# Linear attention and two expert layers: the order of the first head pair's token groups, omega's preparation, and matmuls over zeros at the start

## The chip, the cores and the metric

One Trainium2 chip, one core of it. A NeuronCore has a matrix engine (TensorE, PE in the profile, with its weight loads as PEld), VectorE (DVE), ScalarE (ACT), GpSimd (POOL) and SyncE (SP), which here issues the loads and stores. Each engine works through its own queue in order and waits on semaphores for the others. The metric is the time of one execution on the device in microseconds (us); lower is better.

## The reference

Attention with random features, then a layer with h - tanh(h), then four experts weighted by probabilities. Sizes: batch 2, 8 heads, 576 tokens, head width 64, 128 features; 1152 tokens by 512 channels in both layers.

```python
def phi(x):
    proj = np.einsum('bhsd,md->bhsm', x, omega)
    sq = np.sum(x * x, axis=-1, keepdims=True) / 2.0
    h = proj - sq
    h = h - np.max(h, axis=-1, keepdims=True)
    return np.exp(h) / np.sqrt(m)
q_p, k_p = (phi(q_s), phi(k_s))             # q and k scaled by D**-0.25
kv = np.einsum('bhsm,bhsd->bhmd', k_p, v)
z = np.sum(k_p, axis=2)
num = np.einsum('bhsm,bhmd->bhsd', q_p, kv)
den = np.einsum('bhsm,bhm->bhs', q_p, z)[..., None] + 1e-06
x = num / den                               # 1152 x 512
h = x @ w_in
x = (h - np.tanh(h)) @ w_out
for e in range(4):
    out += p[:, e:e + 1] * (np.maximum(x @ w1[e], 0.0) @ w2[e])
```

## The kernel before

The eight heads are taken as four pairs. A pair's keys are 2 x 576 tokens. In tiles of 128 rows that is nine: four full tiles of each batch, and one tile that holds the last 64 tokens of both batches, the rest. `kn` holds a pair's full tiles (two loads, one for each batch), `kr` the rests of all pairs, `vs0` and `vs1` the values of the even and odd pairs, `qn` and `qr` the queries. SyncE issues every load, in program order; a load into a buffer that is used again waits until the last reader of the buffer is done: the values of pair 2 wait for the products of pair 0 (in two halves, one for each batch), the keys of pair 3 for the transposes of pair 1.

`features` (lines 273 to 306) turns a pair's keys into features in two kinds of step. `transposed` turns four blocks of 128 x 128 at a time by matmuls with `ident` into `psT` (two buffers, line 284) and splits the result into a rounded half `th` (ScalarE, line 71) and the remainder `tl` (VectorE, line 72). `projected` takes one group: two token tiles of both heads, or the rest tile. For each block of 128 columns it does three matmuls of 256 columns (line 296: `th` by `ob0`, `th` by `ob1`, `tl` by `ob0`) into `psP`, which has two buffers; then VectorE takes the maximum (`nm`, line 298) and ScalarE the exponentials into `kf`, one for each tile and head (line 302). The buffer of `psP` comes free behind the last exponential. The list `groups` says in which order tiles are taken: two groups of batch 0, the rest, two groups of batch 1.

`k_products` (line 308) multiplies features and values: 20 products of a pair into `psV` (line 314), each of which is two records in the trace. Behind the keys the queries go through the same features, `psQ` and `psN` are their further steps, and `pse` and `psh` are the first matmuls of the first layer. The weights of that layer come in as `raw` (line 103), are decoded on ScalarE (`y`, line 111) and VectorE (`m`, lines 122, 126, 127) and are split into `wah` and `wal`.

`ob0` and `ob1` are omega's two parts: omega is loaded (`om`), transposed into `pso` (line 251), scaled into `oms` (line 253) and split (lines 71 and 72) into two tiles that were cleared before (line 256).

In the attention a scheduler of the framework sets the order of the instructions on each engine: it goes by the order of the program and by its own estimate of when operands are ready. From the first `psh` on, the order on TensorE, VectorE and ScalarE is the one that is written in the program.

## Time and profile before

| | us |
|---|---|
| median of 3 runs | 681.08 (680.87 to 681.24) |
| the profiled execution | 681.03 |
| its span, first to last instruction | 678.9 |
| TensorE busy (matmuls) | 666.2, 98% |
| weight loads | 621.5, 92% |
| VectorE busy | 529.8, 78% |
| ScalarE busy | 317.5, 47% |

TensorE is busy nearly all the time, so a part of the kernel matters by how much time TensorE loses in it, by waiting or by a slow clock. A row of the time by stage gives, for a stretch from A to B, the busy time of each engine with its number of instructions, then the granted clock, the share of the DMA engines' time and the rate in GB/s. A row of a timeline begins with its start and its duration; several instructions of one kind in a row are merged (x4), and a bracket at its end tells how long the engine had been idle and what ended that.

### The profile page before, as it was taken

The numbers are of one execution on the slowest core, as the hardware profiler recorded it, in microseconds if no ns is written. First come the engines' busy times: TensorE is split into PE (matmuls) and PEld (weight loads), VectorE is DVE, ScalarE is ACT, GpSimd is POOL, SyncE is SP. The second block draws the span as 40 slices with busy tenths as digits, with TensorE's granted clock in tenths as the row PEclk, the third lists the DMA queues.
The fourth block names the chain that finished last, engine by engine and source line by source line (L and its number), as shares of the span: only waits on it lengthen the run. The fifth ranks groups of instructions, "written<-read, shape, count | busy, mean of one in ns | idle before, by whom it ended". The sixth has DMA issues, their size and how long they took to land.

```text
span 678.9 us, 10154 instructions
## 1 busy us (share of the span) xinstructions
PE 666.2 (98%) x4059; PEld 621.5 (92%) x4059; DVE 529.8 (78%) x828; ACT 317.5 (47%) x593; POOL 62.3 (9%) x58
## 2 busy tenths in 40 slices
PE   6999999999999999999999999999999999999997
PEld 5999989999999999998999999998998999999986
DVE  4599889799999988968377777777777777777664
ACT  5699988857767756444122322222232223222120
POOL 1032023413212200100000000000000000000000
PEclk9999999999999999999999999999999999999999
DMA  8953201122322222121001111210202111110004
GB/s 225 281 169 119 67 32 32 32 62 95 94 63 93 78 79 63 31 63 32 1 31 63 32 49 45 63 33 32 63 31 63 32 63 32 36 58 1 1 0 140
DMA packets 42767, 43.73 MB, mean 64 GB/s; under 512 B 5600, under 2 KB 37600, under 8 KB 42720
## 3 DMA queue, kind: packets, MB, share of 16 engines
q1 hardware_dynamic: 42720, 43.08, 20.7%
q8 instruction: 32, 0.52, 0.3%
q14 instruction: 15, 0.12, 0.1%
HBM read 40.72 MB, written 2.36 MB: 63 GB/s over the span
## 4 chain that ended last, share of the span: by engine, by line
PE 79%; DVE 11%; ACT 5%; issue 2%; DMA 2%; SPq 1%; DVEq 0%
PE po L671 29%; PE Y L654 23%; PE po L550 7%; PE psh L437 7%; PE pse L437 4%; PE psP L296 3%; PE psN L348 2%; DVE m L127 1%; DVE m L126 1%; DVE y L451 1%; DVE y L452 1%; DVE y L454 1%; DVE psh L453 1%; ACT y L448 1%; PE psQ L337 1%
## 5 line engine op out<-in xcount | busy, mean ns | idle before, releaser
L677 DVE SCALAR_TENSOR_TENSOR oacc<-po,pr,oacc 128x512 f32<-128x512 f32 (+1 forms) x136 | 101.4, 746 | 34.3 <-PE po L671 33.8
L671 PE MATMUL po<-wbh,hl 128*128 128x512 f32 x290 | 113.0, 389 | 0.4 <-DVE hl L474 0.4
L671 PE MATMUL po<-wbh,hh 128*128 128x512 f32 x290 | 112.9, 389 | 0.1
L671 PE MATMUL po<-wbl,hh 128*128 128x512 f32 x290 | 112.9, 389 | 0.0
L671 PEld LDWEIGHTS po<-wbh,hl 128*128 128x128 f32 x290 | 54.4, 188 | 12.3 <-DVE hl L474 0.8
L671 PEld LDWEIGHTS po<-wbh,hh 128*128 128x128 f32 x290 | 54.7, 188 | 8.2 <-DVE oacc L677 0.3
L842 ACT ACTIVATE hh<-Y 128x576 fp32r<-128x576 f32 x42 | 27.4, 652 | 72.5 <-DVE Y L839 64.0
L671 PEld LDWEIGHTS po<-wbl,hh 128*128 128x128 f32 x290 | 54.4, 188 | 7.5
L550 PE MATMUL po<-hh,wbh 128*128 128x384 f32 x180 | 60.8, 338 | 0.3
L550 PE MATMUL po<-hl,wbh 128*128 128x384 f32 x180 | 60.7, 337 | 0.3 <-DVE hl L456 0.2
L550 PE MATMUL po<-hh,wbl 128*128 128x384 f32 x180 | 60.4, 336 | 0.0
L654 PE MATMUL Y<-y,wah 128*128 128x288 f32 x336 | 57.9, 294 | 0.0
L437 PE MATMUL psh<-x,wah 128*128 128x384 f32 x288 | 57.7, 336 | 0.0
L654 PEld LDWEIGHTS Y<-y,wah 128*128 128x128 f32 x336 | 51.2, 188 | 3.6 <-DVE hl L474 0.3
L437 PEld LDWEIGHTS psh<-x,wah 128*128 128x128 f32 x288 | 50.5, 188 | 0.0
L654 PE MATMUL Y<-Th,wal 128*128 128x288 f32 x224 | 47.9, 295 | 0.0
L654 PE MATMUL Y<-Tl,wah 128*128 128x288 f32 x224 | 47.6, 294 | 0.0
L654 PE MATMUL Y<-Th,wah 128*128 128x288 f32 x224 | 47.6, 293 | 0.0
L842 ACT ACTIVATE hh<-u 128x576 fp32r<-128x576 f32 x14 | 9.6, 687 | 73.5 <-DVE u L839 73.5
L654 PEld LDWEIGHTS Y<-Th,wah 128*128 128x128 f32 x224 | 39.0, 188 | 4.5
L455 ACT ACTIVATE hh<-y 128x1152 fp32r<-128x1152 f32 (+3 forms) x26 | 20.6, 796 | 41.4 <-DVE y L454 41.4
L624 ACT ACTIVATE wah<-y 128x512 fp32r<-128x512 f32 x28 | 17.6, 631 | 41.1 <-DVE y L604 41.1
(138 smaller groups left out, 1472.7 us busy)
## 6 DMA issues: line engine op xcount, KB each, us to landing
raw<-in_moe_w_dram SPq DMA_DIRECT2D x30, 512.0 KB, 3.5
raw<-in_moe_w_in_dram SPq DMA_DIRECT2D x16, 512.0 KB, 3.6
raw<-in_moe_w_out_dram SPq DMA_DIRECT2D x16, 512.0 KB, 3.4
kn<-in_k_dram SPq DMA_DIRECT2D x8, 256.0 KB, 3.9
vs<-in_v_dram SPq DMA_DIRECT2D x8, 256.0 KB, 4.3
qn<-in_q_dram SPq DMA_DIRECT2D x8, 256.0 KB, 4.9
out_dram<-oacc SPq DMA_DIRECT2D x7, 256.0 KB, 2.2
raw<-in_moe_w_dram SPq DMA_DIRECT2D x4, 256.0 KB, 3.2
```

The source lines that it names most:

```text
L126: nc.vector.scalar_tensor_tensor(out=m, in0=self.y.bitcast(I32), scalar=3, in1=m, op0=ALU.logical_shift_left, op1=ALU.bitwise_or)
L127: nc.vector.scalar_tensor_tensor(out=m, in0=self.up, scalar=SIGN, in1=m, op0=ALU.bitwise_and, op1=ALU.bitwise_or)
L296: nc.tensor.matmul(ps[:, i].rearrange("p a m -> p (a m)"), x[:, c], o, start=j == 0, stop=j == 2)
L348: nc.tensor.matmul(ps[:, j, h, :ZC], qt[g][:, j, h, :], kvz[p][:, t // (TB + 1), h, :], start=True, stop=True)
L437: nc.tensor.matmul(ph[i, j][:, n, :CH] if bank is None else bank, w[:, c], x[:, n * CH:(n + 1) * CH] if bank is None else x[:, n], start=z ...
L455: h=lambda: act.activation(hh, y, AF.Copy),
L550: nc.tensor.matmul(po[:, :CH], w[:, r], g[:, s], start=j == 0 and z == 0, stop=j == NJ - 1 and z == 2,)
L624: nc.scalar.activation(w[0], src, AF.Copy)
L654: nc.tensor.matmul(ps[:, m, :HN // 2], w[:, kk], b[:, m * HN // 2:(m + 1) * HN // 2], start=first and kk == 0 and z == 0, stop=kk == 1 and ...
L671: nc.tensor.matmul(po, g[:, s], w[:, cols], start=j == 0 and z == 0, stop=j == 1 and z == 2)
L677: nc.vector.scalar_tensor_tensor(out=acc, in0=po, scalar=pr[:, t, e:e + 1], in1=acc, op0=ALU.mult, op1=ALU.add)
L842: nc.scalar.activation(halves(gs[NA + q, f][0][:, h * HN:(h + 1) * HN]), x, AF.Relu)
```

## The change

Three edits, all at the start of the attention. `kgroups` gives pair 0 another order of groups: the two of batch 0, the two of batch 1, then the rest; the other pairs keep theirs. Omega's transpose, scaling and split are put under the scheduler's high priority, behind the clearing of `ob`. And twelve matmuls of 256 columns (`busy`, six ahead of omega's transpose and six behind) over a tile of zeros go to a bank of PSUM that nothing reads (`idle`); the tile `zero` is cleared by VectorE first. Of the tag `n` in PSUM `idle` takes one of two buffers, which `psV` uses next.

```diff
--- before.py
+++ after.py
@@ -246,22 +246,36 @@
     load_v(0)
     kn.append(load_k(1))
     load_v(1)
-
-    pso = ps_t.tile([P, 512], F32, tag="t", name="pso")
-    nc.tensor.transpose(pso[:, :P], om.rearrange("p j d -> p (j d)"), ident)
-    oms = kp.tile([P, P], F32, name="oms", bufs=1)
-    nc.scalar.mul(oms, pso[:, :P], scale)
+    zero = kp.tile([P, 2 * P], F32R, name="zero", bufs=1)
+    nc.vector.memset(zero.bitcast(F32), 0.0)
+    idle = ps_n.tile([P, 512], F32, tag="n", name="idle")
+
+    def busy(n):
+
+        for _ in range(n):
+            nc.tensor.matmul(idle[:, :2 * P], zero[:, :P], zero, start=True, stop=True)
+
+
     ob = [ac.tile([P, 2 * P], F32R, name=f"ob{a}") for a in range(2)]
     for a in range(2):
         nc.vector.memset(ob[a].bitcast(F32), 0.0)
-    for j in range(2):
-        r, c = slice(j * D, (j + 1) * D), slice(j * P, (j + 1) * P)
-        split(ob[0][r, c], ob[1][r, c], oms[r, :])
+    pso = ps_t.tile([P, 512], F32, tag="t", name="pso")
+    with tc.high_priority():
+        busy(6)
+        nc.tensor.transpose(pso[:, :P], om.rearrange("p j d -> p (j d)"), ident)
+        busy(6)
+        oms = kp.tile([P, P], F32, name="oms", bufs=1)
+        nc.scalar.mul(oms, pso[:, :P], scale)
+        for j in range(2):
+            r, c = slice(j * D, (j + 1) * D), slice(j * P, (j + 1) * P)
+            split(ob[0][r, c], ob[1][r, c], oms[r, :])
     qn = ac.tile([P, B, H, TD], F32, name="qn")
     kvz = [ac.tile([P, B, 2, ZC], F32, name=f"kvz{p}") for p in range(NP)]
 
 
     groups = [(0, 2), (2, 2), (TB, 1), (TB + 1, 2), (TB + 3, 2)]
+
+    kgroups = [groups[:2] + groups[3:] + groups[2:3]] + [groups] * (NP - 1)
 
     def blocks(full, rest, t0, n):
 
@@ -374,7 +388,7 @@
     post = []
     for p in range(NP):
         kf = kp.tile([P, NT, 2, M], F32, tag="xf", name="kf")
-        T, R = features(lambda b, h: kn[p][:, b, h], kr[:, 2 * p:2 * p + 2, :].rearrange("p h d -> p (h d)"), groups, kf, kp)
+        T, R = features(lambda b, h: kn[p][:, b, h], kr[:, 2 * p:2 * p + 2, :].rearrange("p h d -> p (h d)"), kgroups[p], kf, kp)
         interleave(T[:2] + R[:2] + T[2:] + R[2:], post)
         post = k_products(p, kf)
         if p + 2 < NP:
```

Lines below `kgroups` are 14 further down in the changed program (line 284 is 298, 296 is 310, 314 is 328, 302 is 316, 298 is 312). The scheduler orders the attention anew. From the first `psh` of the first layer on, TensorE's order is the same in both.

TensorE at the start, before: omega (`pso`), four transposes of pair 0's first batch, then the rest `kr` with three of the second batch.

```order
L251 MATMUL pso_126<-ident_67,om_97 128x128
L284 MATMUL psT_146<-ident_67,kn_99 128x128 x4
L284 MATMUL psT_153<-ident_67,kr_102 128x128
L284 MATMUL psT_153<-ident_67,kn_99 128x128 x3
L296 MATMUL psP_160<-ob0_130,th_144 128x256
L296 MATMUL psP_173<-ob0_130,th_144 128x256
L284 MATMUL psT_186<-ident_67,kn_99 128x128
L296 MATMUL psP_160<-ob1_131,th_144 128x256
```

And with the change, the twelve passes first:

```order
L256 MATMUL idle_128<-zero_126 128x256 x12
L265 MATMUL pso_133<-ident_67,om_97 128x128
L298 MATMUL psT_161<-ident_67,kn_99 128x128 x4
L298 MATMUL psT_168<-ident_67,kn_99 128x128 x4
L310 MATMUL psP_175<-ob0_129,th_159 128x256
L310 MATMUL psP_188<-ob0_129,th_159 128x256
L298 MATMUL psT_201<-ident_67,kr_102 128x128
L310 MATMUL psP_175<-ob1_130,th_159 128x256
```

All eight transposes of full tiles now stand ahead of that of `kr`, and the two first projections too.

TensorE further on, where pair 0's last groups meet pair 1 (keys `kn_119` and features `kf_143` before, `kf_158` now) and pair 2 (`kn_240`). Before:

```order
L296 MATMUL psP_211<-ob0_130,th_144 128x256
L296 MATMUL psP_211<-ob1_131,th_144 128x256
L296 MATMUL psP_211<-ob0_130,tl_145 128x256
L296 MATMUL psP_211<-ob0_130,th_144 128x256
L296 MATMUL psP_211<-ob1_131,th_144 128x256
L296 MATMUL psP_211<-ob0_130,tl_145 128x256
L314 MATMUL psV_224<-vs0_105,kf_143 128x128 x4
L284 MATMUL psT_281<-ident_67,kn_119 128x128
L314 MATMUL psV_224<-vs0_105,kf_143 128x128
```

With the change:

```order
L298 MATMUL psT_296<-ident_67,kn_119 128x128
L310 MATMUL psP_231<-ob0_129,th_159 128x256
L310 MATMUL psP_231<-ob1_130,th_159 128x256
L310 MATMUL psP_231<-ob0_129,tl_160 128x256
L298 MATMUL psT_379<-ident_67,kn_240 128x128 x4
L310 MATMUL psP_265<-ob0_129,th_244 128x256
L310 MATMUL psP_265<-ob1_130,th_244 128x256
L310 MATMUL psP_265<-ob0_129,tl_245 128x256
L328 MATMUL psV_239<-vs0_105,kf_158 128x128
```

The rest group (three projections, `psP_231`) is the last of pair 0 now, and the transposes of pair 2's first batch (`psT_379`) stand ahead of pair 1's first projections (`psP_265`); before they stood 20 rows further down.

SyncE's loads from the queries' rests (`qr`) to the first weights (`raw`), before:

```order
L203 DMA qr_338<-in_q_dram 64x8x64 x2
L199 DMA qn_138<-in_q_dram 128x2x256 x2
L199 DMA vs0_105<-in_v_dram 128x2x256
L237 DMA vs0_105<-in_v_dram 64x2x64
L199 DMA kn_335<-in_k_dram 128x2x256 x2
L199 DMA qn_138<-in_q_dram 128x2x256 x2
L199 DMA vs0_105<-in_v_dram 128x2x256
L237 DMA vs0_105<-in_v_dram 64x2x64
L199 DMA qn_138<-in_q_dram 128x2x256 x4
L103 DMA raw_349<-in_moe_w_in_dram 128x4x128
```

With the change:

```order
L203 DMA qr_353<-in_q_dram 64x8x64 x2
L199 DMA kn_350<-in_k_dram 128x2x256 x2
L199 DMA qn_153<-in_q_dram 128x2x256 x3
L199 DMA vs0_105<-in_v_dram 128x2x256
L237 DMA vs0_105<-in_v_dram 64x2x64
L199 DMA qn_153<-in_q_dram 128x2x256 x3
L199 DMA vs0_105<-in_v_dram 128x2x256
L237 DMA vs0_105<-in_v_dram 64x2x64
L199 DMA qn_153<-in_q_dram 128x2x256 x2
L103 DMA raw_364<-in_moe_w_in_dram 128x4x128
```

The keys of pair 3 (`kn_335`, now `kn_350`) and one more load of queries moved ahead of the first values of pair 2 (`vs0`). ScalarE around the first use of `raw`, before:

```order
L302 ACTIVATE kf_361<-psP_383,nm_390 128x128 x4
L302 ACTIVATE kf_361<-psP_401,nm_408 128x128 x3
L111 ACTIVATE y_351<-raw_349 128x512
L302 ACTIVATE kf_361<-psP_401,nm_408 128x128
L302 ACTIVATE kf_361<-psP_423,nm_427 128x128 x2
L71 ACTIVATE th_481<-psT_483 128x512
```

With the change:

```order
L316 ACTIVATE kf_376<-psP_416,nm_423 128x128 x2
L111 ACTIVATE y_366<-raw_364 128x512
L316 ACTIVATE kf_376<-psP_416,nm_423 128x128 x2
L316 ACTIVATE kf_376<-psP_438,nm_442 128x128 x2
L71 ACTIVATE wah_372<-m_368 128x512
L111 ACTIVATE y_485<-raw_483 128x512
```

`y` stood ahead of the last of a group's four exponentials and now stands ahead of the last two of them.

## Rows read from the trace of the kernel before

**Rows 1.** Time by stage: window, busy PE, PEld, DVE, ACT, POOL, clock, DMA.

```profile
11.00:32.00 21.00, 19.88 (x166) 19.21 (x165) 11.86 (x22) 15.46 (x53) 0.00 (x0) 1.00 0.92 274
32.00:51.00 19.00, 18.48 (x157) 17.69 (x155) 18.96 (x33) 17.92 (x52) 6.53 (x5) 1.00 0.60 181
51.00:117.00 66.00, 66.00 (x508) 61.75 (x509) 59.56 (x154) 60.20 (x156) 14.55 (x13) 1.00 0.20 64
117.00:679.00 562.00, 556.94 (x3214) 518.56 (x3213) 436.28 (x612) 220.39 (x328) 38.95 (x28) 1.00 0.16 50
```

**Rows 2.** Timeline of TensorE, 2 to 12 us: start, duration, instruction.

```profile
4.52 1.11 PE L284 MATMUL psT<-ident,kn 128*128 128x128 f32 x4 [1.28 <-DMA kn<-in_k_dram]
7.62 0.45 PE L284 MATMUL psT<-ident,kr 128*128 128x128 f32 x1 [1.99 <-DMA kr<-in_k_dram]
...
10.21 0.41 PE L296 MATMUL psP<-ob,th 128*128 128x256 f32 x1
10.43 0.41 PE L296 MATMUL psP<-ob,tl 128*128 128x256 f32 x1
...
11.09 0.60 PE L284 MATMUL psT<-ident,kn 128*128 128x128 f32 x4
11.52 0.27 PE L284 MATMUL psT<-ident,kr 128*128 128x128 f32 x1
```

**Rows 3.** DMA issues of pair 1's keys, at 6.30 and 6.94: us to landing.

```profile
kn<-in_k_dram SPq DMA_DIRECT2D x1, 256.0 KB, 3.7
...
kn<-in_k_dram SPq DMA_DIRECT2D x1, 256.0 KB, 4.1
```

**Rows 4.** Timeline of all engines, 0 to 60 us: VectorE and ScalarE.

```profile
6.91 0.59 DVE L72 TENSOR_TENSOR ob<-oms,ob 64x128 fp32r<-64x128 f32 x2
...
10.45 1.52 DVE L298 TENSOR_REDUCE nm<-psP 128x4 f32<-128x512 f32 x2 [0.19 <-PE psP L296]
...
11.18 2.17 ACT L302 ACTIVATE kf<-psP,nm 128x128 f32<-128x128 f32 x8 [1.51 <-DVE nm L298]
```

**Rows 5.** Timeline of SyncE's queue, 12 to 32 us.

```profile
12.45 1.13 SPq L199 DMA_DIRECT2D qn<-in_q_dram  x2
16.27 0.37 SPq L199 DMA_DIRECT2D vs<-in_v_dram  x1
...
22.49 2.12 SPq L199 DMA_DIRECT2D qn<-in_q_dram  x4
24.66 0.47 SPq L103 DMA_DIRECT2D raw<-in_moe_w_in_dram  x1
```

**Rows 6.** Time by stage, shorter stretches; the last number is GB/s.

```profile
16.00:18.00 2.00, 2.00 (x21) 2.00 (x19) 1.11 (x3) 1.64 (x7) 0.00 (x0) 1.00 0.67 167
...
28.00:32.00 4.00, 2.92 (x25) 2.67 (x24) 1.69 (x5) 2.90 (x11) 0.00 (x0) 1.00 1.07 338
```

**Rows 7.** DMA issue of the first weights at 24.66: us to landing.

```profile
raw<-in_moe_w_in_dram SPq DMA_DIRECT2D x1, 512.0 KB, 6.0
```

**Rows 8.** The page's DMA issues: all weights of that kind, median to landing.

```profile
raw<-in_moe_w_in_dram SPq DMA_DIRECT2D x16, 512.0 KB, 3.6
```

**Rows 9.** Timeline of ScalarE, 24 to 35 us.

```profile
30.70 0.67 ACT L111 ACTIVATE y<-raw 128x512 f32<-128x512 f32 x1 [1.10 <-DMA raw<-in_moe_w_in_dram]
31.27 0.86 ACT L302 ACTIVATE kf<-psP,nm 128x128 f32<-128x128 f32 x3
```

**Rows 10.** Timeline of TensorE, 26 to 36 us.

```profile
31.68 0.50 PE L296 MATMUL psP<-ob,th 128*128 128x256 f32 x2 [1.08 <-ACT kf L302]
...
33.16 1.05 PE L314 MATMUL psV<-vs,kf 128*128 128x128 f32 x8
34.05 0.27 PE L284 MATMUL psT<-ident,kr 128*128 128x128 f32 x1
```

**Rows 11.** The chain of waits, in order of time: start, us, what.

```profile
30.70 0.68 ACT y L111
...
49.16 0.64 ACT wbh L71
```

## The prediction

> **What bounds the kernel now.** I read the time by stage first [rows 1]. From 117 us on TensorE is busy for 556.94 of 562 us, and the change leaves its order there alone, so that part only shifts as a block: whatever the attention gains or loses before 117 us is the whole effect. The profiled execution took 681.03 us, its span 678.9 and 2.13 around it; the median of the three runs is 681.08, so sums against the profiled one need no correction. Between 11 and 32 us TensorE is busy for 19.88 of 21 us, from 32 to 51 for 18.48 of 19, beside VectorE's 18.96 of 19. Three engines are nearly full, and a gain of one reaches the end only if the others follow.
>
> Next the start [rows 2]. The first transposes begin at 4.52 us, when the keys land. The transpose of the rest (`kr`) waits 1.99 us more, to 7.62, and everything behind it in TensorE's queue waits too. From there TensorE works on, but slowly: the passes of 256 columns at 10.21 and 10.43 are 0.21 us apart, which is 1.2 GHz; the four transposes from 11.09 to 11.52 take 0.11 each, the full clock. The column of the granted clock says 1.00 throughout, so here only the spacing shows the two levels.
>
> Then the keys of pair 1. Their two loads are issued from 6.30 and 6.94 us and take 3.7 and 4.1 us [rows 3], so they land at about 10.0 and 11.04. Before, their transposes begin at 11.09, 0.05 us behind the second landing. **This is the gate at the front:** the slow clock and the wait for `kr` were paid inside the time which that load takes anyway.
>
> **The change part by part.** The passes over zeros: 12 of 0.21 us are 2.5 us, from about 1.2 us (behind a first memset) to 3.8. They delay omega's transpose by about 1 us, which has slack: the ScalarE copies of `ob` stand behind the first `th` copy in both orders, and VectorE's parts of `ob` were done at 7.5 [rows 4]. They end 0.7 us ahead of the keys at 4.52, so they cost nothing; if they began 0.8 us later, they would push the first transposes.
>
> Omega's priority: it moves omega's parts past nothing on ScalarE or VectorE (the same copies stand ahead of them), so I count it as zero.
>
> The rest group last: the second four transposes of pair 0 no longer stand behind `kr`. They need keys issued half a microsecond behind the first, so they run from about 5.4 us in time that was idle. At 7.62 one transpose and ten projections are left. At either clock they end by 10.0 (11 x 0.21 = 2.3) and then the keys of pair 1 are waited for, to 10.0 and 11.04. At 11.06 five transposes more than before are done: 5 x 0.11 = **0.55 us gained**.
>
> From 11 to 22.5 us I set the new order against the rows' durations: transposes 0.11 and matmuls of the products 0.11 each (eight from 33.16 to 34.05, two records to a product), a group of six projections 0.7 (twelve from 31.68 to 33.16) [rows 10], a maximum 0.7 and a group's four exponentials 1.1 [rows 4]. The first rest group now is the fifth, so a full group (six passes, maximum, four exponentials) must go through in its place before the two projection buffers come free. `psP_231` reaches TensorE's head at 13.8 and waits for the exponentials of `psP_205`, which begin only behind the late transposes of 11.06: 11.83 + 0.7 projections, 0.9 to the end of its maximum, 1.1 exponentials, 14.6. Then the transposes of pair 2 (`psT_379`), which stood 20 rows later, need the copy that empties their buffer (15.3), and `psP_265` needs the exponentials of `psP_218` (15.9). Waits of 0.8 + 0.3 + 0.2 = 1.3 us, against about 0.7 us of scattered waiting in the old order between 11.09 and 22.53. So the 0.55 is spent: at the point where pair 0's products are done, and pair 1's projections too, I have the new kernel at 22.6 against 22.5. **Front: 0, between -0.5 and +0.6.**
>
> The load queue is what is left. Before, SP issues the second q load by 13.58 us and stands still until 16.27 [rows 5], for a v load that waits for the tenth product; behind it wait the keys of pair 3. DMA then falls to 167 GB/s in 16 to 18 us, against 338 in 28 to 32 [rows 6]. Now the keys of pair 3 and three q loads stand ahead of that v load; they wait only for pair 1's last transpose, about 14.3. So the queue doesn't run dry. It matters for the first expert-weight load `raw`: issued at 24.66 [rows 5], 6.0 us to landing [rows 7], 30.68. ScalarE's `y` from it stands **in the middle of a group's exponentials**, so ScalarE idles 1.10 us up to 30.70 [rows 9], and TensorE, which needs the projection buffer, 1.08 up to 31.68 [rows 10]. In the new order `y` again stands inside such a group, with two exponentials behind it instead of one, and four transposes and two products (0.88 us) that TensorE had done ahead now stand behind the stop. With the landing at R, TensorE resumes at R + 1.0 + 0.25, with 0.88 us more to do. The gain there is 31.68 - 0.88 - 1.25 - R = 29.55 - R, at most 1.6, since TensorE gets there at 29.2.
>
> R has two ends: issue at about 24.2 (after the twentieth product at 22.0, the v rest and two q loads) plus 3.6, the median landing of such loads [rows 8], 27.8; and 30.7, as before. The missing 171 GB/s of 16 to 18 us is 0.34 MB, 1.0 us at 338; some more is slack up to 28. I take R = 28.8, nearer the middle: TensorE gains 0.75 there, VectorE, which stood waiting for the same load, 1.9.
>
> From 32 to 51 us the chain of waits runs on VectorE and ScalarE without a break, from `y` at 30.70 to `wbh` at 49.16 [rows 11]; so that stretch starts 1.9 us earlier, while TensorE is 0.75 earlier and has 0.5 of idle there to lose. Between 0.75 and 1.9 I take **1.1 us**, nearer to TensorE's end. From 51 to 117 TensorE is busy for 66.00 of 66 us [rows 1] and only rows of neighbouring steps change places: 0, give or take 0.5. Sum: 681.03 - 0 - 1.1 = **679.9**.
>
> **Rivals.** *Loads early.* If R is 28.2 or less and VectorE leads, TensorE makes up its 0.5 of idle: 1.4 to 2.3 us, about 679.1. For it speaks the empty queue at 16 us; against it, that TensorE had only 0.5 us of idle to give back up to 51.
>
> *The front gain carries through.* If TensorE comes out of the start at the full clock and the others keep pace, fifteen passes at 0.21 instead of 0.11 (1.6 us) and the 0.55 us both count: 681.03 - 2.15 = 678.9. Against it stands the landing at 11.04, which nothing in the change moves. The Trainium skill, "TensorE: Matmul & The Clock Gate", Part 1 on the clock gate, says that the default state is throttled and activity releases it; by that rule the passes would earn this 1.6 us. The rows agree on the two levels, and by them the time is spent waiting for the load instead.
>
> *Nothing arrives.* The order from 51 on, or new waits at the front, eat the 1.1 us: 681.0, within 0.4.
>
> *Loads late, slower.* The keys of pair 3 and three q loads now go ahead of the v load, and the tenth product comes at 18.0 instead of 16.2. If the queue is full anyway, R isn't earlier, and `y` with `wah` and a second `y` behind it holds the exponentials. The point is R = 29.55: above it the new kernel loses. At R = 31.0 it loses 1.45: 682.5. Against it: as many bytes ahead of `raw` as before, issued earlier.
>
> **How the numbers follow.** A measurement of this kernel can tell about 0.2%, 1.36 us, from no change. Forecast (gain 0.4 to 1.36) 0.37 at 679.9; loads early 0.32 at 679.1; front carries 0.08 at 678.9; nothing arrives 0.15 at 681.0; loads late 0.08 at 682.5. Faster by over 0.2%: 0.32 + 0.08 = 0.40. Within: 0.37 + 0.15 = 0.52. Slower: 0.08. The range 678.5 to 681.5 takes in the first four, with 0.4 below the front's case and 0.5 above the fourth for the order after 51; outside lie the slower case and some of the edges.
>
> **What would show it.** In the changed profile: passes over zeros done before 4.5; transposes of pair 0 at about 5.4; one at 7.62 for `kr`; pair 1's transposes still at 10.0 and 11.04 to 11.1 (if they are earlier, the gate is wrong and the front carries). Waits of TensorE for exponentials near 14 and 16 us. No stretch near 167 GB/s at 16 to 18 us; `raw` issued near 24.2 and landing near 28.8; `y` on ScalarE right behind it, and the first hidden projection (`psh`) about 1.1 us earlier. It is wrong if `raw` lands at 30 or later, or if the stretch from 51 to 117 changes its length by more than 0.5 us.

## The result and the profile after

The changed kernel is **slower**: 685.84 us against 681.09 for the kernel before, a ratio of 1.0065 with an interval of 1.0052 to 1.0078. A second measurement of the same two kernels gave 684.83 (683.79 to 685.37) against 681.38, 1.0046 (1.0032 to 1.0061). One of the first executions, the one that was profiled, took 1103.58 us at a granted clock of 0.555 from 5.6 us to its end, as no other run did and for a cause that is open; it stands outside the ratio, and the profile shown here is of an execution of the second measurement (685.17 us, span 683.1, against 681.03 and 678.9 before).

Time by stage of the changed kernel, columns as in [rows 1]:

```profile
11.00:32.00 21.00, 18.48 (x152) 17.44 (x152) 11.13 (x21) 14.06 (x46) 0.00 (x0) 1.00 0.92 277
32.00:51.00 19.00, 19.00 (x151) 18.60 (x151) 17.69 (x30) 16.12 (x46) 5.12 (x4) 0.91 0.58 174
51.00:117.00 66.00, 64.87 (x497) 60.35 (x497) 60.45 (x153) 60.18 (x157) 13.96 (x11) 1.00 0.21 65
121.00:127.00 6.00, 4.69 (x30) 4.05 (x29) 3.79 (x10) 4.95 (x14) 3.01 (x4) 1.00 0.00 1
127.00:683.00 556.00, 551.25 (x3179) 513.48 (x3177) 431.78 (x602) 214.34 (x312) 34.65 (x24) 1.00 0.16 50
```

Four things differ from [rows 1]. TensorE is busy for 18.48 of the 21 us from 11 to 32, against 19.88. From 32 to 51 us it is busy all the time and yet does fewer instructions (151, before 157), because the granted clock is 0.91. From 51 to 117 us it idles 1.13 us, where it idled nothing. And 1.3 us are missing just behind the first `psh`, in a stretch that the prediction took as fixed.

**The start** (timeline of TensorE, as [rows 2]):

```profile
1.20 2.93 PE L256 MATMUL idle<-zero 128*128 128x256 f32 x12 [1.20 <-DVE zero L250]
4.13 1.71 PE L298 MATMUL psT<-ident,kn 128*128 128x128 f32 x8
7.38 0.30 PE L298 MATMUL psT<-ident,kr 128*128 128x128 f32 x1 [0.44 <-DMA kr<-in_k_dram]
10.37 0.63 PE L298 MATMUL psT<-ident,kn 128*128 128x128 f32 x4 [1.50 <-DMA kn<-in_k_dram]
14.37 0.30 PE L298 MATMUL psT<-ident,kn 128*128 128x128 f32 x1 [0.33 <-DVE tl L72]
```

The passes are done when the keys come, all eight transposes run at once, and behind the transpose of `kr` and the projections TensorE waits 1.50 us for pair 1's keys.

**Around the first weights** (timelines of TensorE and ScalarE, then SyncE's issue and its us to landing; to be laid beside [rows 5, 7, 9, 10]):

```profile
28.64 1.05 PE L328 MATMUL psV<-vs,kf 128*128 128x128 f32 x8
31.60 0.50 PE L310 MATMUL psP<-ob,th 128*128 128x256 f32 x2 [1.91 <-ACT kf L316]
32.67 0.78 PE L310 MATMUL psP<-ob,th 128*128 128x256 f32 x2
34.94 1.70 PE L328 MATMUL psV<-vs,kf 128*128 128x128 f32 x10
36.92 1.28 PE L328 MATMUL psV<-vs,kf 128*128 128x128 f32 x10
...
30.37 0.68 ACT L111 ACTIVATE y<-raw 128x512 f32<-128x512 f32 x1 [1.76 <-DMA raw<-in_moe_w_in_dram]
...
24.52 0.47 SPq L103 DMA_DIRECT2D raw<-in_moe_w_in_dram  x1
...
raw<-in_moe_w_in_dram SPq DMA_DIRECT2D x1, 512.0 KB, 5.8
```

The load is issued at 24.52, 0.14 us earlier than before, and lands 5.8 us later, at 30.34. `y` follows at once, and TensorE resumes at 31.60, after a stop of 1.91 us (before 1.08). Behind it two passes take 0.78 us where 0.50 is usual, and ten records of products 1.70 where 1.28 is usual. The time by stage names the reason in its clock column, the third from the end:

```profile
32.40:35.80 3.40, 3.40 (x19) 3.40 (x17) 2.54 (x6) 2.90 (x9) 1.28 (x1) 0.50 0.67 188
35.80:40.00 4.20, 4.20 (x39) 4.20 (x39) 4.20 (x7) 3.22 (x8) 1.30 (x1) 1.00 0.83 244
```

For 3.4 us behind the stop TensorE runs at 1.2 GHz. Before, the stop of 1.08 us had no such stretch.

**From 51 to 61 us** the largest wait is for the remainder `tl` of a block whose `th` stands on ScalarE behind a weight's `y` (TensorE, ScalarE, VectorE):

```profile
55.57 0.41 PE L351 MATMUL psQ<-ident,qf 128*128 128x128 f32 x2 [0.62 <-DVE tl L72]
...
52.66 0.68 ACT L111 ACTIVATE y<-raw 128x512 f32<-128x512 f32 x1
53.69 0.62 ACT L71 ACTIVATE th<-psT 128x512 fp32r<-128x512 f32 x1
...
54.75 0.68 DVE L72 TENSOR_TENSOR tl<-psT,th 128x512 fp32r<-128x512 f32 x1
```

ScalarE is done with `th` at 54.31, and VectorE, busy with other rows, starts `tl` 0.44 us later.

**Behind the first `psh`** (TensorE, ScalarE, GpSimd):

```profile
123.08 0.51 PE L451 MATMUL pse<-x,wah 128*128 128x256 f32 x2 [1.14 <-DVE y L468]
...
120.70 0.51 ACT L462 ACTIVATE y<-u,ca 128x256 f32<-128x256 f32 x1 [0.97 <-POOL hl L470]
...
118.40 1.30 POOL L72 TENSOR_TENSOR wal<-m,wah 128x512 fp32r<-128x512 f32 x1 [1.36 <-ACT wah L71]
119.65 1.01 POOL L470 TENSOR_TENSOR hl<-y,hh 128x384 fp32r<-128x384 f32 x1
```

The last early matmuls (`pse`) wait 1.14 us for VectorE's `y`, which waits for ScalarE's, which waits for GpSimd's `hl`, which stands behind a weight's low part `wal`. A sentence ahead of the prediction has to be corrected here: among the `psh` TensorE's order is the written one, but the scheduler places the last twelve `pse` between them, before behind 16 of them and now behind 9.

**The loss by place.** To compare traces whose instructions stand in different order, I count the work: each of TensorE's records by the usual spacing of its form in the trace of before. The table gives how much later than the kernel before a run has done the same work, at points named by the time of before (us). The passes over zeros are left out. Each row is one execution. At 33 and 40 us instructions change places from run to run, and these two columns are good to about 0.3 us (0.5 in the row of y behind its group); the others to 0.1.

| profile of | 22.5 | 28 | 33 | 40 | 50 | 60 | 116 | 124 | 400 |
|---|---|---|---|---|---|---|---|---|---|
| changed | 0.45 | 0.10 | 1.80 | 2.01 | 1.92 | 2.96 | 2.92 | 4.32 | 4.26 |
| new order, no passes | 2.05 | 1.70 | 2.95 | 3.66 | 3.58 | 4.61 | 4.58 | 5.98 | 5.91 |
| old order, passes | -0.28 | -0.29 | -0.49 | -0.50 | -0.25 | -0.24 | -0.24 | -0.24 | -0.17 |
| changed, first weights first | 0.59 | 0.51 | -0.84 | 0.21 | 0.57 | 1.65 | 0.99 | 2.56 | 2.49 |
| changed, y behind its group | 1.99 | 1.64 | 1.00 | 1.62 | 2.24 | 4.58 | 5.47 | 6.88 | 6.82 |
| changed, last pse behind | 0.49 | 0.15 | 1.92 | 2.31 | 2.23 | 3.27 | 3.25 | 4.66 | 4.59 |
| that, and weights' parts behind | 0.53 | 0.19 | 0.83 | 1.26 | 1.15 | 2.19 | 2.16 | 2.39 | 2.34 |
| changed, keys first | -1.00 | -1.35 | -0.91 | -0.58 | -0.67 | 0.37 | 0.34 | 1.76 | 1.75 |
| all three | -0.64 | -0.98 | -0.33 | 0.34 | 0.26 | 1.29 | 1.26 | 1.48 | 1.39 |
| before, keys first | 0.47 | 0.49 | 2.64 | 2.62 | 2.25 | 2.30 | 2.30 | 2.29 | 2.27 |

In the changed kernel's row the front ends level (0.10 at 28 us), 1.8 are lost between 28 and 50 us, 1.0 between 50 and 60, and 1.4 between 116 and 124. These are the three places that the experiments had to explain.

### The profile page after: what moved, and what is told of

Same layout as the page of the kernel before. It is cut to its first block, busy times and chain, and to the rows that moved or that the text cites. A ratio compares the mean times of both kernels' runs of the same rounds, so it can differ in the third digit from the quotient of the medians.

```text
span 1101.7 us, 10172 instructions
## 1 busy us (share of the span) xinstructions
PE 1094.9 (99%) x4071; PEld 829.6 (75%) x4071; DVE 527.1 (48%) x829; ACT 323.4 (29%) x593; POOL 65.2 (6%) x58
## 4 chain that ended last, share of the span: by engine, by line
PE 99%; SPq 0%; DMA 0%; issue 0%; DVE 0%
PE po L685 30%; PE Y L668 23%; PE psh L451 15%; PE po L564 14%; PE pse L451 4%; PE psP L310 4%; PE psV L328 3%; PE psN L362 2%; PE psQ L351 1%; PE psT L298 1%; PE psh L564 1%; PE psX L377 1%; DMA kn<-in_k_dram 0%; PE psN L366 0%; SPq L199 0%; SPq L203 0%
## 5 line engine op out<-in xcount | busy, mean ns | idle before, releaser
L685 PE MATMUL po<-wbh,hl 128*128 128x512 f32 x290 | 166.7, 575 | 0.0
L685 PE MATMUL po<-wbl,hh 128*128 128x512 f32 x290 | 166.4, 574 | 0.0
L685 PE MATMUL po<-wbh,hh 128*128 128x512 f32 x290 | 165.7, 572 | 0.0
L685 PEld LDWEIGHTS po<-wbh,hl 128*128 128x128 f32 x290 | 63.5, 219 | 47.7 <-issue 28.8
L451 PE MATMUL psh<-x,wah 128*128 128x384 f32 x288 | 92.2, 479 | 0.0
L668 PE MATMUL Y<-y,wah 128*128 128x288 f32 x336 | 88.5, 407 | 0.0
L564 PE MATMUL po<-hl,wbh 128*128 128x384 f32 x180 | 86.7, 482 | 0.0
L564 PE MATMUL po<-hh,wbl 128*128 128x384 f32 x180 | 86.4, 480 | 0.0
L564 PE MATMUL po<-hh,wbh 128*128 128x384 f32 x180 | 85.9, 477 | 0.0
L668 PE MATMUL Y<-y,wal 128*128 128x288 f32 x168 | 52.6, 408 | 0.0
L451 PE MATMUL psh<-x,wal 128*128 128x384 f32 x144 | 50.9, 480 | 0.0
```

The source lines that it names most:

```text
L451: nc.tensor.matmul(ph[i, j][:, n, :CH] if bank is None else bank, w[:, c], x[:, n * CH:(n + 1) * CH] if bank is None else x[:, n], start=z ...
L564: nc.tensor.matmul(po[:, :CH], w[:, r], g[:, s], start=j == 0 and z == 0, stop=j == NJ - 1 and z == 2,)
L668: nc.tensor.matmul(ps[:, m, :HN // 2], w[:, kk], b[:, m * HN // 2:(m + 1) * HN // 2], start=first and kk == 0 and z == 0, stop=kk == 1 and ...
L685: nc.tensor.matmul(po, g[:, s], w[:, cols], start=j == 0 and z == 0, stop=j == 1 and z == 2)
```

## The experiments

**Which edit loses.** The kernel again; the new order of groups without the passes and the priority; and the old order with passes and priority. The priority moves nothing: with it and the passes, in the old order, every engine's queue is that of the kernel before, apart from the passes and their memset.

```diff
+    kgroups = [groups[:2] + groups[3:] + groups[2:3]] + [groups] * (NP - 1)   # alone
...
+    kgroups = [groups] * NP      # with busy(6) twice, zero and high_priority
```

> The changed kernel as it is, for a second set of times and a second profile. Theory A (the passes over zeros disturb TensorE's clock later on): about 685 us again, the profile's mean granted clock below 1, with a stretch after the start where the spacing of matmuls falls back to that of 1.2 GHz; now and then an execution over 1000 us. Theory B (the new order loses by waits, as the rival with late loads said): about 685 us with the clock at 1.000 and the loss in waits before 117 us.

> The changed order of pair 0's groups alone: every queue has the order of the changed kernel, without the twelve passes over zeros and their memset. Theory A: the order is worth what the prediction said, 679.5 to 681, no execution far above, granted clock 1.000. Theory B: about 685.

> The kernel before with the twelve passes over zeros (and their memset) ahead of omega's transpose, and nothing else moved. Theory A: 684 to 686 and sometimes far more, with a mean granted clock below 1. Theory B: 681, within 0.5, as the passes end before the first keys land.

Measured: 684.83 (ratio 1.0046), 685.84 (1.0063, 1.0042 to 1.0083) and 680.91 (0.9999, 0.9987 to 1.0010). So the order costs the time, about 4.5 us alone, and passes in the old order cost and gain nothing. In the new order the median with passes is 1.0 us lower, though the two intervals overlap, and the first measurement of the changed kernel had the median of the run without passes, 685.84. So the times show no sure gain from the passes. The profiles show where one can come from; these are two passes of one form on TensorE in the new order without passes:

```profile
13.01 0.78 PE L298 MATMUL psP<-ob,th 128*128 128x256 f32 x2
14.67 0.48 PE L298 MATMUL psP<-ob,th 128*128 128x256 f32 x2
```

Without passes TensorE runs at half clock to 14.1 us, in the kernel before to 10.8. In the changed kernel the passes had brought the full clock at 5.1 us. By the table the two executions differ by 1.6 us at 22.5 us. It is the clock behind the landing of pair 1's keys that counts there: the run with its first weights first, below, has passes too and fell back to half clock from 7.5 to 10.9 us. Its projections are slow, but its transposes of pair 1 begin at 10.38 us as in the changed kernel, and at 22.5 us it is only 0.14 us behind that. The profiled execution of the old order with passes fell back as well, from 7.9 to 11.3 us.

The Trainium skill, "TensorE: Matmul & The Clock Gate", Part 1, says that the default state is throttled and that activity releases it. The trace agrees with it at the start (full clock from 5.1 us with the passes, from 14.1 us without).

**The stop at 30 us.** The first weights loaded first of all; twelve more products put into the stop (their result is read by nobody); `y` moved to the next pair's steps, in both kernels.

```diff
+            first = load_a(0, 0)          # ahead of the queries; scaled and joined there too
...
+                for _ in range(12):       # ahead of the fourth group of pair 2
+                    nc.tensor.matmul(warm[:, :P], kf[:, 2, 1, :], kf[:, 2, 1, :], start=True, stop=True)
...
-    EARLY = {1: [(load_a, wa, 0, 0)], 2: [(load_a, wa, 0, 1)]}
+    EARLY = {2: [(load_a, wa, 0, 0), (load_a, wa, 0, 1)]}
```

> The changed kernel with the load of the first weights (raw) issued ahead of the queries' loads, right behind the keys of pair 2, and its decoding left where it stands in the program. Theory C (TensorE's wait of 1.9 us near 29.7 us for exponentials that stand behind y on ScalarE, which waits for raw, and the fall of TensorE's clock for 3.41 us that follows it, are the loss): no wait over 0.5 us near 30 us, clock at 1.00 from 12 us to the end, 681 to 682. Rival D (the new order loses by waits that stand elsewhere, at 52 to 61 and 121 us): those waits stay and the time is 684 to 685.

> The changed kernel with 12 extra products (24 records of 0.11 us, 2.7 us) of finished features into an unused bank, placed by their operands where TensorE waits near 29 us; nothing reads them. They displace four products (0.89 us) behind the wait. Theory C: the clock stays at 1.00 through 32 to 36 us, which saves 1.4 to 1.5 us, less the 0.9: about 684.3, and psP behind the wait starts at about 31.6 as before. If the clock's fall has nothing to do with the wait: it falls at the same place and the time is about 685.7.

> The changed kernel with the first weights taken one pair later in the program, so that y stands behind all four exponentials of the group on ScalarE, not ahead of its last two. Theory C: the projection at 29.7 us no longer waits for raw, the wait moves to the next one and shrinks to under 1 us, the clock stays at 1.00: 682 to 683. Rival D: 684 to 685.

> The kernel before with the same edit (first weights one pair later, y behind all four exponentials). Theory C: of its wait of 1.1 us near 30.6 us most goes: 680.2 to 680.8. Rival D: 681.1, as the weights' chain on VectorE then starts later by what TensorE saved.

Measured: 684.05 (1.0040), 689.63 (1.0116), 687.96 (1.0101), and 683.9 (1.0039) for the kernel before with later decoding. Loading the weights first takes the stop away: the table has that run at 0.21 at 40 us, where the changed kernel has 2.01. Waits of 0.75 and 0.34 us come instead, behind `th` and `tl`; then 1.1 us are lost from 50 to 60 and 1.6 behind 116:

```profile
34.66 0.50 PE L310 MATMUL psP<-ob,th 128*128 128x256 f32 x2 [0.75 <-ACT th L71]
35.72 0.39 PE L310 MATMUL psP<-ob,tl 128*128 128x256 f32 x1 [0.34 <-DVE tl L72]
```

So the stop is the late load's, and it is not the whole loss. Filling the stop (24 records of `warm`) only moved the trouble: TensorE waited behind it, then twice more, and the clock fell there instead, for 6.7 us. As the scheduler also ordered the steps behind the filling anew, this run is no clean test of what the filling does to the clock:

```profile
28.80 2.94 PE L397 MATMUL warm<-kf 128*128 128x128 f32 x24
32.48 0.50 PE L310 MATMUL psP<-ob,th 128*128 128x256 f32 x2 [0.74 <-ACT kf L316]
...
38.86 0.50 PE L310 MATMUL psP<-ob,th 128*128 128x256 f32 x2 [1.59 <-ACT th L71]
40.69 0.58 PE L310 MATMUL psP<-ob,tl 128*128 128x256 f32 x1 [1.33 <-DVE tl L72]
...
39.60:46.30 6.70, 5.61 (x26) 5.61 (x27) 4.71 (x9) 3.84 (x11) 0.15 (x1) 0.50 0.36 111
```

Later decoding lost 2.6 us in the old order and 3.1 in the new one, at different places. Counted as in the table, the new order with it loses 3.5 us between 28 and 40 us (changed kernel 1.9), in a stop of 2.67 us with half clock behind it, and 2.3 from 50 to 60 (changed kernel 1.0). The old order is level there (0.21 late at 60 us, 0.31 at 116) and loses 2.2 us from 116 to 124, where these two waits stand:

```profile
121.25 0.51 PE L437 MATMUL pse<-x,wah 128*128 128x256 f32 x2 [1.05 <-DVE y L454]
...
124.68 0.45 PE L550 MATMUL po<-hh,wbh 128*128 128x384 f32 x1 [1.05 <-DVE y L454]
```

So the place behind 117 us, where the changed kernel loses 1.4, suffers in the old order too when the attention is ordered anew, and the time of such a run doesn't judge the edit at 30 us.

**The place of `y`.** `behind` puts one instruction after another in their engine's queue. On ScalarE `y` queued behind all four exponentials of its group, in both kernels; and the kernel before with its first weights loaded first.

```diff
+    behind(ys[0], exps[43])
```

> The changed kernel, with the first weights' scaling (y) on ScalarE queued behind all four exponentials of the group in which it stood, not ahead of the last two; the scheduler orders the rest anew around it, and the loads keep their order. TensorE's buffer then no longer waits for the load. Theory R (the place of y in front of a load that lands at 30.3 is what stops TensorE for 1.9 us and lets its clock fall for 3.4 us, 1.45 us of cost): no stop over 0.8 us from 28 to 33 us, no stretch at half clock there, and 2 to 3 us back: 682 to 683. Rival D (VectorE and ScalarE are behind by the load anyway, so TensorE stops a little later on the exponentials behind y): a stop of 1 us or more between 31 and 36 us, and 684 to 686.

> The kernel before with the same rule: y of the first weights behind all four exponentials of its group, where it stood ahead of the last. In the kernel before that place cost 1.08 us of TensorE without a fall of the clock. Theory R: up to 1 us back, 680.0 to 681.0. Rival D: the wait comes back behind y, 681 to 682.5. This is also the counterpart of the run of the changed kernel with y behind its group: by theory R the difference between the two orders falls from 4.4 to 2 us or less; by D it stays above 3.

> The kernel before with the first weights loaded and scaled early, the same edit as the run of the changed kernel with its weights first (684.05). Theory R: the old order keeps its 681 or gains up to 1 us (680 to 681.3), so that with no load to wait for near 30 us the new order still loses 2.5 to 4 us: then the rest of the loss is in the order of the later steps and not in the load. Rival Q (loading the weights first costs the queue of loads 2 us by itself): 682.5 to 684, and the new order with its weights first is level with the old one.

Measured: 687.1 (1.0088), 685.09 (1.0055), 685.23 (1.0066), all worse. The time alone speaks against the theory, the place doesn't. In the first the stop is down to 0.44 us, and from 28 to 50 us it loses 0.6 us (1.64 and 2.24 in the table), where the changed kernel loses 1.8. But this execution ran at half clock from 10.5 to 13.8 us (1.5 us at the front), and the reordered steps behind lost 2.3 from 50 to 60 us and more to the end.

```profile
32.80 0.51 PE L316 MATMUL psP<-ob,th 128*128 128x256 f32 x2 [0.44 <-ACT kf L322]
...
10.50:13.80 3.30, 3.08 (x15) 3.11 (x16) 0.00 (x0) 2.36 (x7) 0.00 (x0) 0.50 0.97 288
```

In the kernel before, `y` behind its group still left a stop of 2.21 us at 33.05, since the group behind `y` waited (rival D). Yet counted as in the table it is only 0.6 us late at 60 us and 1.3 at 116; 4.5 us are lost from 116 to 130 us, in waits of 0.95 and 1.96 us and at half clock from 127.3 to 130.7. With its weights first, `y` met the load too early and stood in front of four exponentials for 4.2 us; TensorE waited 3.4:

```profile
18.41 0.68 ACT L111 ACTIVATE y<-raw 128x512 f32<-128x512 f32 x1 [4.21 <-DMA raw<-in_moe_w_in_dram]
...
19.39 1.00 PE L314 MATMUL psV<-vs,kf 128*128 128x128 f32 x4 [3.44 <-ACT kf L302]
```

It is the same mechanism at another place; as a counterpart of the changed kernel with weights first it tells nothing.

**Behind 117 us.** The last `pse` put behind 16 `psh`, as before; then also two weights' parts (`wah`, `wal`) behind `hh` and `hl` of the early blocks, as before. In the first no other queue differs, in the second ScalarE's and GpSimd's alone.

```diff
+        behind(pse12[0], psh[15])
...
+    for w, e in ((NJ + 1, 6), (NJ + 2, 7)):
+        for a, b in zip(halves["wa"][w], parts[e]):
+            behind(a, b)
```

> The changed kernel, with one thing moved: the last group of early matmuls (pse) stands behind 16 hidden ones (psh), as in the kernel before, and not behind 9. Nothing else in any queue differs from the changed kernel. In the profile of the changed kernel TensorE waits 1.14 us at 121.6 us for VectorE's y, ahead of that pse; the seven psh moved ahead of it are 7 x 0.174 = 1.2 us of work for that wait. Theory S (the loss behind 117 us is this place alone): the wait is filled, about 1.1 us come back, 683.6 to 684.0 against the changed kernel's 684.8 to 685.8, and the profile shows no wait over 0.3 us at the first psh. Rival W (VectorE is that late anyway, and the next reader waits in its place, at po or the next psh): no difference, 684.8 to 685.8, and the wait stands a few us later.

> The kernel of the run with the last early matmuls behind (685.95), and beside that two weight parts of the next step (wah on ScalarE, wal on GpSimd) queued behind the sixth and the seventh early block's hh and hl, as they stand in the kernel before; in the changed order each stands one block earlier. TensorE's, VectorE's and the loads' queues are the same. In the profile GpSimd's wal (1.3 us) from 118.7 us holds hl up to 120.0, ScalarE's y waits 0.97 us for that hl at 121.0, and TensorE's po then waits 1.41 us for VectorE's y. Theory P (the loss behind 117 us is the place of the weights' parts in front of hl): the waits go, 0.8 to 1.4 us come back, 684.5 to 685.2. Rival L (the chains of the last blocks are late by their own start, a block later than in the kernel before): 685.5 to 686.5, and the wait of po stays above 1 us.

Measured: 685.95 (1.0073, 1.0061 to 1.0085) and 683.26 (1.0035, 1.0022 to 1.0047). The first alone gives nothing: the wait moves on to `po`, as rival W had it. With the weights' parts behind, GpSimd does `hl` ahead of `wal`, and 0.42 us of that wait are left. First the run with `pse` alone, then the other (TensorE, GpSimd, time by stage):

```profile
126.86 0.44 PE L570 MATMUL po<-hh,wbh 128*128 128x384 f32 x1 [1.41 <-DVE y L474]
```

```profile
124.57 0.44 PE L576 MATMUL po<-hh,wbh 128*128 128x384 f32 x1 [0.42 <-DVE y L476]
...
117.69 1.01 POOL L478 TENSOR_TENSOR hl<-y,hh 128x384 fp32r<-128x384 f32 x1 [1.40 <-ACT hh L477]
119.89 1.29 POOL L75 TENSOR_TENSOR wal<-m,wah 128x512 fp32r<-128x512 f32 x1 [1.20 <-issue]
...
32.00:36.00 4.00, 4.00 (x38) 4.00 (x37) 3.77 (x7) 3.54 (x12) 1.28 (x1) 1.00 0.76 227
```

From 116 to 124 us the loss falls from 1.41 to 0.23 us. So the two weights' parts held the end of the attention: on GpSimd, which is busy for 9% of the span, `wal` kept ScalarE's `y` waiting 0.97 us for `hl` in the changed kernel, and on ScalarE `wah` stood ahead of `hh`. The two were moved together, so the share of each is open.

The time fell by 2.7 us, more than expected. Between the two profiled executions (685.57 and 683.24 us) the table accounts for it, with 1.2 us at the end and 1.1 from 28 to 50 us. There the run with `pse` alone stops for 2.14 us and has half clock behind it; the other stops for 1.93 and keeps the full clock, as the last row above says:

```profile
31.88 0.50 PE L313 MATMUL psP<-ob,th 128*128 128x256 f32 x2 [2.14 <-ACT kf L319]
```

```profile
31.70 0.50 PE L315 MATMUL psP<-ob,th 128*128 128x256 f32 x2 [1.93 <-ACT kf L321]
```

Their instructions up to there are the same, and 0.2 us is the longer stop, so **the clock's fall cost about 0.9 us**. The changed kernel gives the same: with its stop of 1.91 us and the fall it loses 1.8 us from 28 to 50, where the run with the weights' parts behind loses 1.0. Two other executions without a fall (keys first; all three) lose 0.7 and 1.2 us there, so the figure is good to about 0.3. The medians are not explained by it: of the executions with `pse` alone, the two with a mean clock of 0.999 or more took 685.25 and 685.95 us.

**The gate at the front.** The loads of pair 1's keys ahead of pair 0's values: in the changed kernel, in the old order with passes, and in the kernel before. Nothing else moves on any queue.

```diff
-    load_v(0)
     kn.append(load_k(1))
+    load_v(0)
     load_v(1)
```

> The changed kernel with one thing moved: the loads of pair 1's keys are issued ahead of pair 0's values. No other queue changes. Tests the gate of the prediction at 11.04 us. In the changed kernel TensorE waits 1.5 us for those keys up to 10.4. Theory G (the landing is the gate at the front): that wait goes, pair 0's part runs up to 1.5 us earlier, 22.5 us becomes 21.0 to 21.8, and as the first weights are issued behind it they land about 1 us earlier too: 683.3 to 684.2. Rival H (TensorE waits for the values or for exponentials instead, or the landing of the first weights stays at 30.3 and the front's gain ends there): 684.6 to 686.

> The kernel before with the passes, and the loads of pair 1's keys ahead of pair 0's values. No other queue differs from the run of the old order with passes (680.91). Theory G: with the clock released early and the keys there by about 8.7 us, the front gains up to 1 us, of which the wait for the first weights near 31 us takes a part: 680.0 to 680.7. Rival H: 680.9 to 682, the front waits for pair 0's values instead.

> The kernel before with the loads of pair 1's keys ahead of pair 0's values and nothing else. Without passes the slow clock to 10.8 us paces the front, and the wait for those keys is 0.05 us in the kernel before. Theory G: nothing gained at the front by the load alone, 680.7 to 681.4; so what the run with passes and keys first has beyond this one is the clock's. Rival H: the values come late for the first products, 681.5 to 683.

Measured: 683.27 (1.0040, 1.0024 to 1.0055), 680.91 (0.9994, 0.9984 to 1.0004), 681.09 (0.9993, 0.9984 to 1.0002). In the changed kernel the wait of 1.50 us is gone, TensorE stops again at the weights, which land at 28.72 (issued at 23.07), and resumes at 29.97:

```profile
8.52 0.60 PE L298 MATMUL psT<-ident,kn 128*128 128x128 f32 x4
...
29.97 0.50 PE L310 MATMUL psP<-ob,th 128*128 128x256 f32 x2 [1.73 <-ACT kf L316]
...
23.07 0.47 SPq L103 DMA_DIRECT2D raw<-in_moe_w_in_dram  x1
```

So pair 1's keys gate the front of the new order, and in the traces the gain is carried through: 1.45 us at 22.5 us in the table and 2.5 at 400, where this execution was spared the clock's fall as well. The medians differ by 1.56 us, though the intervals of the two ratios overlap. In the old order the same move gives nothing that can be measured; but neither of its profiled executions had early keys at the full clock (with passes it waited 2.60 us for `kr` and was at half clock from 8.2 to 11.6 us, without them to 13.0). The profiled execution of the kernel before with keys first (682.97 us) shows that the old order can lose its clock in the same way, behind a stop of 2.26 us:

```profile
33.35 0.71 PE L296 MATMUL psP<-ob,th 128*128 128x256 f32 x2 [2.26 <-ACT kf L302]
...
33.50:36.80 3.30, 3.30 (x16) 3.30 (x17) 2.53 (x5) 2.72 (x9) 1.14 (x1) 0.50 1.02 337
```

**All together.** Keys first, last `pse` and weights' parts behind; that and the eighth weight's `y` behind the `th` that it held at 52.7 us; and the first with the load of the first weights ahead of the queries' loads.

```diff
+    behind(ys[7], ths[14])
...
+            first = load_a(0, 0)          # at pair 1, ahead of rests(q, ...); used where it was
```

> The changed kernel with both edits that gave time back: pair 1's keys loaded first (683.27) and the tail's order as in the kernel before (last early matmuls behind 16 hidden ones, two weight parts one block later, 683.26). Theory: the two places are 100 us apart and add up: against 684.8 to 685.8, 1.5 to 2 us for the keys and 1.1 to 1.4 for the tail, 681.4 to 682.6; left over against the kernel before are the 1 us of waits at 50 to 60 us and, in executions where the clock falls behind the wait for the first weights, about 1 us more. Rival: the tail starts earlier but its chains do not, and half of its 1.3 us comes back as a wait: 682.3 to 683.

> The same, and the scaling (y) of the eighth weight tile, which in the changed order stands ahead of the first qt and the th behind it at 52.7 us on ScalarE, queued behind that th; it comes to stand some ten instructions later, where the kernel before has it too. In the profile of the changed kernel TensorE waits 0.78 us at 54.7 us for VectorE's tl of that th, part of the 1.0 us that the new order loses from 50 to 60 us. Theory Y (that decoding in front of th is what makes the wait): 0.6 to 1.0 us back against the run without it, 680.6 to 681.9, and no wait over 0.3 us at 52 to 56 us. Rival: the wait is VectorE's, which is busy through 50 to 56 us: no difference, 681.4 to 682.6.

> As the run with the keys first and the tail's order, and the load of the first weights issued ahead of the queries' loads, behind the keys of pair 2. The scheduler orders the steps from there to 117 us anew. Theory R: the weights land well before 28 us, and the stop of 1.9 us with the clock's fall behind it goes, 1 to 2.5 us back, 679.5 to 681.2. Rival V (the load takes 1.5 us of the queue ahead of pair 2's values or pair 3's keys, and the steps are ordered worse): a wait of 1 us or more at another place, 681.5 to 684.

Measured: 682.67 (1.0021, 1.0008 to 1.0034), 682.52 (1.0021, 1.0009 to 1.0032) and 682.22 (1.0015, 1.0005 to 1.0026). The first lies just above what its theory allowed (682.6 at most) and inside its rival (682.3 to 683). The late `y` did not take the wait away: TensorE still waits 0.90 us for `tl`, so theory Y falls; VectorE's row of work there is the likelier cause, and that was not tested by itself. That edit also had the scheduler order VectorE's and TensorE's steps from 58 to 103 us anew. With the weights' load early the stop at 30 us is gone, and a wait of 1.14 us stands at 39.1 us in its place; the time lies in the range of rival V, though the stop went as theory R had it. In order, the two waits:

```profile
53.34 0.41 PE L358 MATMUL psQ<-ident,qf 128*128 128x128 f32 x2 [0.90 <-DVE tl L75]
```

```profile
39.13 0.50 PE L315 MATMUL psP<-ob,th 128*128 128x256 f32 x2 [1.14 <-ACT kf L321]
```

No version beats the kernel before by more than its measurement can tell, and these three are still slower by 0.15 to 0.21%.

## Why the prediction was wrong

It said 679.9 with a range to 681.5, and gave slower by over 0.2% a chance of 0.08. The time is 4.9 to 5.9 us above the forecast.

**The passes and the priority.** As forecast, the passes end ahead of the keys and the priority moves nothing. But in the new order they are worth 1.6 us in the one pair of traces. I had argued that the slow clock is paid inside the load's time in both orders. Without passes the new order has pair 1's keys at 10.56 us and goes on behind them at half clock, up to 14.1 us. In these two executions the full clock was needed to end level; the passes don't secure it (the run with `y` behind its group has them, and fell back to half clock from 10.5 to 13.8 us). In the prediction, fifteen passes at 0.21 instead of 0.11 us come to 1.5 us and not 1.6.

**The gate and the front.** Right for the new order: the keys of pair 1 gate the front, and moving them alone gained 1.5 us in the traces. For the kernel before it was not shown: there TensorE works without a wait from 7.62 us to the transposes at 11.09, so the slow clock fills the same time, and keys first changed nothing (0.9993). The level at 22.5 us was missed by 0.35 (0.45 late, forecast 0.1), and at 28 us it is 0.10.

**The load's time R, the step that gave the sign.** I took 28.8 from bounds of 27.8 and 30.7; it is 30.34, near the upper end. Two parts of it failed. The load took 5.8 us, nearly as before [rows 7], not something nearer to the median of 3.6 [rows 8]. That median is of later loads: in the kernel before the four of this kind that were issued before 32 us took 4.7 to 6.7 us, the eleven from 53 us on 3.5 to 4.3. And the missing 171 GB/s of 16 to 18 us did come (312 in the row below, against 167 in [rows 6]), but did not reach this load: over 11 to 32 us the rate is 277, and was 274. The hole of before had been made up elsewhere.

```profile
16.00:18.00 2.00, 2.00 (x19) 1.93 (x17) 1.02 (x3) 1.08 (x4) 0.00 (x0) 1.00 0.99 312
```

What follows from R was right to 0.01 us: TensorE resumes at R + 1.25 = 31.59 (measured 31.60) with 0.88 us more to do, and by 29.55 - R the place loses 0.79 us. An execution without the clock's fall bears it out: with its weights at 30.44 us, the run with the weights' parts behind loses 1.0 us from 28 to 50, where 29.55 - R gives 0.9. That is the rival with the late loads, which I had given 0.08 since as many bytes stand ahead as before. They do, but that argues for the same R, and the point 29.55 lies below the R of before.

**The clock behind the stop, not in the sum.** A stop of 1.91 us instead of 1.08 was followed by 3.4 us at half clock, about 0.9 us lost. I had used the clock for the start alone. Not every execution has this fall: in the second measurement the two with a mean granted clock of 0.999 and 1.000 took 683.79 and 684.50 us, the two with 0.996 took 685.17 and 685.37.

**32 to 51, gain of 1.1.** It hung on R and turned into the loss above. **51 to 117, zero give or take 0.5:** it lost 1.0. That TensorE was busy all the time before says nothing on how a new order fits the other engines. All runs of the new order in the table lose 1.0 or more between 50 and 60 us, those of the old order nothing; which instruction makes it is left open.

**After 117 only a block.** Wrong by 1.4 us: the scheduler's order on GpSimd and ScalarE there decides when the last early blocks are done. With two weights' parts put back, it is 0.23.

The sum by places is 0.1 + 0.9 (the late load) + 0.9 (the clock) + 1.0 + 1.4 = 4.3 us, against 4.2 between the spans. The one rival on the slower side had the mechanism of the second term only.

## What to carry to other kernels

When a scheduler orders a stretch anew, a small edit at its start is a new draw for the whole stretch: price each queue up to its end, the lightly used engine among them, before calling a part fixed. For the same reason, see in the trace where such a run lost before its time is taken as a verdict on the edit. A load's landing is to be taken from the same load in the same traffic, not from the median of its kind; and ask at which landing time the sign changes before choosing a value. Passes that keep TensorE busy can pay where dense work would else follow at the slow clock (1.6 us here in one pair of traces), and pay nothing where that work waits for a load anyway.

## What the hardware showed

The length of a stop near 30 us did not decide whether the granted clock fell behind it. It went to half for 3.4 us behind stops of 1.91 us (changed), 1.94 (new order, no passes), 2.14 (last `pse` behind), 2.26 (before, keys first) and 2.67 (changed, later decoding). It did not behind stops of 1.73 (changed, keys first), 1.91 (late `y`), 1.93 (weights' parts behind; all three) and 2.21 (before, `y` behind its group). What decides is open. By the table, the difference between the run with last `pse` behind and the one with the weights' parts behind, with and without the fall, is 1.05 us at 40 us and 1.09 at 116, so what is lost reaches the end of the attention.

Over the twelve executions with all three edits, the eight with a mean granted clock of 0.999 or more average 682.0 us, two at 0.996 to 0.997 average 683.5, and two at 0.994 average 685.1. The mean does not say where in the program the clock fell.

The passes brought the full clock at 4.1 to 7.1 us in twelve of the thirteen profiles with passes that reach it, and at 10.6 in the last (weights' load early). In four of the twelve it went back to half for 3.4 us before 14 us. Without passes it came at 10.3 to 14.1 us.

The clock column says 1.00 ahead of its first record even where the rows run at half clock (the run without passes, 5 to 14 us), so the start has to be read from the spacing of the passes.
